# Attention and an MLP woven on one core: a round of maxima moved ahead of the score pair behind the products with v, and gaps of other lengths

## The chip, the core and the metric

The kernel runs on one core of a Trainium2 chip. TensorE (PE in the profile; PEld is its weight load) multiplies matrices, VectorE (DVE) and ScalarE (ACT) read its results from PSUM, GpSimd (POOL) works on SBUF alone, and SyncE (SP) issues most transfers. The metric is the device time of one execution in microseconds (us), the median of several runs. Lower is better.

## What is computed

Attention with 32 heads of 18 columns over 2048 tokens, and a channel MLP on the same tokens, mixed by a gate for each token:

```python
qkv = (x @ wqkv).reshape(B, S, 3, H, Dh)             # S 2048, D 576, H 32, Dh 18
p = softmax(einsum("bhqd,bhkd->bhqk", q, k) * scale)
a = einsum("bhqk,bhkd->bhqd", p, v) -> (B, S, D) @ wo
h = gelu(layernorm(x) @ w1 + b1)                     # F 4608
b = h @ w2 + b2
g = sigmoid((x * gate_w).sum(-1))
out = g * a + (1 - g) * b
```

## The kernel before

A first stage (about 250 us) projects q, k and v and normalises x. Then comes the main loop (lines 1273 to 1309), on which everything below turns; its last periods and a tail behind it hold the projection with wo.

**The loop.** 32 units (a pair of heads and half of the queries) of 16 steps each. A step is one block of 128 keys against 1024 queries. Two steps, an even and an odd one, make a period: from one block of products with v to the next. TensorE's order is the order in which the program is written, and into the loop's own work the MLP's matmuls are woven in pieces.

- **Score pair** (`s2`, line 243): two matmuls (L251) for two heads, side by side on the two halves of the array's rows, 512 queries, into the tile `pss`. Its pool `ps_s2` (line 1051) has one buffer of two banks. One ACTIVATE (L253) takes exp of all 1024 columns. A step has two such pairs, so a period has four: one ahead of the products with v, one behind them, and two in the odd step. A pair cannot begin before the exp of the pair ahead has read `pss`.
- **Products with v** (`pv`, line 257): 16 matmul records (L268) once in a period, on column tiles of 32, where all other matmuls of the loop run on row tiles of 64.
- **Round of maxima** (`s1_round`, line 192): exp needs the maximum of each row, so the scores of a later unit are computed once ahead: two matmuls (L202) into two of the three banks of `ps_s1` (line 93), and two VectorE reductions (L204), each of which frees its bank. A period has four rounds: 1024 in all.
- **Up slots** (`h_pair`, line 478): two matmuls (L502), 27 slots for one pair of hidden tiles. **Output slots** (`out_pair`, line 596): two matmuls (L630), 24 slots for 128 tokens. At slot 12 the two halves swap their column halves ("turn"): a semaphore wait on TensorE, and ahead of it one round of maxima is lent (`lend_round`, line 317); the round that the loop would put next is left out then (`loop_round`, line 322).

**The gaps.** `fill` (line 1249) is called three times in a period: with share 0 at the end of the even step, with share 1 in the middle of the odd one, with share 2 at its end. While rounds are left it runs one piece of the MLP (`atom`, line 730), up to the next cut. The sets `ends` (lines 495 to 499 and 609) say after which slots a piece is cut. With lines 499 and 609 a period holds 24 output slots in pieces of 7, 8 and 9, or up slots in pieces of 4, 5, 5 and then 4, 5, 4. Where an up pair is run in one period, its pieces are 9, 9 and 9.

**The order in an even step**: a round, the score pair, the products with v, the second score pair, a round, the gap (lines 1288 to 1309, with the round behind `s2(u, kc, 1)` at line 1307). In an odd step: a round, the score pair, the gap, a round, the score pair, the gap. In the first 8 steps, line 1299 puts one round more behind the products with v, ahead of the second score pair.

Of the kernel before, what the change touches and what calls it, by code (L numbers as in the profile page):

```python
# [58 lines left out]
def gated_mix_kernel(ctx: ExitStack, tc: tile.TileContext, x, wqkv, wo, w1, b1, w2, b2, gate_w, out):  # L59
# [39 lines left out]
    def psum(pool):  # L99
        return pool.tile([P, TB], F32, name="ps")  # L100
# [18 lines left out]
    def defer(n, fn):  # L119
        later.append((slot[0] + n, fn))  # L120
# [49 lines left out]
    def load_q(u):  # L170
        pair, half = unit(u)
        qa = QA[u % 3]
        for h in range(2):
            d0 = (2 * pair + h) * DH
            for i, part in enumerate((0, 0, 1)):
                r = 64 * h + i * DH
                dma_r(nc.sync, qa[r:r + DH, :], qk_scr[part, d0:d0 + DH, half * HALF:(half + 1) * HALF])

    def load_k(pair, c0=0, c1=S):
        ka = KA[pair % 3]  # L180
        for h in range(2):
            d0 = D + (2 * pair + h) * DH
            for i, part in enumerate((0, 1, 0)):
                r = 64 * h + i * DH
                dma_r(nc.sync, ka[r:r + DH, c0:c1], qk_scr[part, d0:d0 + DH, c0:c1])

    def load_v(pair):
        nc.sync.dma_start(VT[pair % 2], v_scr[:, :, pair, :].rearrange("k p e -> p k e"))
# [54 lines left out]
    def s2(u, kc, qb):  # L243
        qa, ka = QA[u % 3], KA[UNITS[u][0] % 3]
        n = u * NT + kc
        if n < 2 and qb == 0:
            RING.insert(n, pp.tile([P, 2, 2, TB], F32, name="p"))
        ps = ps_s2.tile([P, 2, TB], F32, name="pss")
        for h in range(2):
            r0 = 64 * h  # L250
            nc.tensor.matmul(ps[:, h, :], ka[r0:r0 + 56, kc * P:(kc + 1) * P], qa[r0:r0 + 56, qb * TB:(qb + 1) * TB],  # L251
                             start=True, stop=True)
        nc.scalar.activation(RING[n % 3][:, qb], ps, AF.Exp, scale=SCALE)  # L253
# [3 lines left out]
    def pv(n):  # L257

        u, kc = divmod(n, NT)
        if kc == 0:  # L260
            OB[u] = psum(ps_o)
        v = VT[UNITS[u][0] % 2]
        for c in (n, n + 1):
            for qb in range(2):
                for h in range(2):
                    r = 32 * (2 * h + qb)
                    k = c % NT
                    nc.tensor.matmul(OB[u][r:r + 32, :], v[:, k, 19 * h:19 * h + 32], RING[c % 3][:, qb, h, :],  # L268
                                     start=(k == 0), stop=(k == NT - 1))
        if kc == NT - 2:  # L270
            o_store(u, OB.pop(u))
# [35 lines left out]
    def next_round():  # L307
        if rounds:
            u, r = rounds.pop()
            s1_round(u, r)  # L310
            if r == NR - 1:
                defer(1, lambda: s1_finish(u))
# [4 lines left out]
    def lend_round():  # L317
        if rounds and not lent[0]:
            next_round()
            lent[0] = 1  # L320

    def loop_round():
        if lent[0]:
            lent[0] = 0
        else:
            next_round()

    def mlp():
# [90 lines left out]
        def ready(table, key):  # L419
            while key not in table:  # L420
                bg.pop(0)[1]()
            return table[key]
# [35 lines left out]
        def cuts(n, pieces):  # L458

            return {(k * n + pieces - 1) // pieces for k in range(1, pieces)}  # L460
# [3 lines left out]
        def free_pool():  # L464

            if rounds:
                return ps_w
            turns[0] += 1
            return (ps_s1, ps_w)[(turns[0] - 1) // 2 % 2]
# [8 lines left out]
        def h_pair(q, last, inner=False):  # L478
# [16 lines left out]
            ends = cuts(27, (5, 5, 4)[piece[0]] if last else (3, 5, 4)[piece[0]])  # L495
            if (last or spent[0] > behind[0] + AHEAD) and piece[0] == 0 and not late:

                ends = {4, 9, 14, 18, 23}
            for k, (w_, s_, c) in enumerate(slots):
                for h in range(2):  # L500
                    r = slice(64 * h, 64 * h + 64)
# [94 lines left out]
        def out_pair(i, t, acc):  # L596

            tb, g = seq[i]
            tok = slice(t * P, (t + 1) * P)
            cs = [slice(nn * ND, (nn + 1) * ND) for nn in range(2)]  # L600
            bare = not rounds

            def add(ps, base):
                for nn in range(2):
                    dst = acc[:, t, cs[nn]]
                    nc.vector.scalar_tensor_tensor(dst, ps[nn][:, :ND], 0.5, b2b[:, cs[nn]] if base else dst,  # L606
                                                   op0=ALU.mult, op1=ALU.add)
            ps = [psum(free_pool()) for _ in range(2)]
            ends = {7, 15} if piece[0] == 0 else cuts(24, (3, 2, 1)[piece[0]])
            k = 0  # L610
            for turn in range(2):
                if turn == 1 and bare:
                    add(ps, g == 0)
                    ps = [psum(free_pool()) for _ in range(2)]
                elif turn == 1:
                    if 3 * G not in ends:
                        lend_round()
                    turned[0] += 2
                    nc.tensor.wait_ge(turn_sem, turned[0])
                for j in ORDER:  # L620
                    while (i, j) not in HT:
                        cut[0] = 3
                        yield 0
                    hh, hl = HT[i, j]
                    w_ = ready(W2, (i * (G // 2) + j // 2, j % 2))
                    for h_, p_ in ((hh, 0), (hh, 1), (hl, 0)):
                        for h in (0, 1) if turn == 0 else (1, 0):
                            r = slice(64 * h, 64 * h + 64)
                            nn = h ^ turn
                            mm = nc.tensor.matmul(ps[nn][:, :ND], h_[r, tok], w_[p_][r, cs[nn]],  # L630
                                                  start=(k == 0 or bare and k == 3 * G), stop=(k == 6 * G - 1 or bare and k == 3 * G - 1))
                            if bare:
                                continue
                            if k == 3 * G - 1:
                                mm.then_inc(turn_sem, 1)
                                tc.no_tile_sem_insts.add(mm.ins.name)
                                tc.add_to_no_dep_group(f"turn{turned[0]}", mm.ins)
                            elif k == 3 * G and h == 0:
                                tc.declare_fence(mm.ins, group=f"turn{turned[0] - 2}")
                        k += 1  # L640
                        if k < 6 * G:
                            if k in ends:
                                cut[0] = 1
                            yield 131
            add(ps, g == 0 and not bare)
            if g == NG - 1:
                tt = TBS[tb] * 4 + t
                nc.gpsimd.tensor_scalar(acc[:, t, :], acc[:, t, :], gate1[:, tt:tt + 1], 1.0, op0=ALU.mult, op1=ALU.mult)
                defer(12 if tb < NB - 1 else 4, lambda: nc.sync.dma_start(b_scr[tt * P:(tt + 1) * P, :], acc[:, t, :]))
            cut[0] = 2  # L650
            yield 131
# [74 lines left out]
    piece = [0]  # L726
# [546 lines left out]
    for u in range(NU):  # L1273
        for kc in range(NT):
            step = u * NT + kc
            if kc == 1:
                if u + 2 < NU:
                    load_q(u + 2)
                if u % 2 == 0 and u // 2 + 1 < NPAIR - 1:
                    load_k(u // 2 + 1)  # L1280
                    load_v(u // 2 + 1)
                elif u == NU - 5:
                    load_k(NPAIR - 1)
                elif u == NU - 4:
                    load_v(NPAIR - 1)
            at[0] = step

            loop_round()
            s2(u, kc, 0)
            run_due(462.0)  # L1290
            if kc % 2:
                fill(step, 1)
            elif step > 0:
                pv(step - 2)
                while ROWS:
                    ROWS.pop(0)()
                run_due(2080.0)
                if step <= 2 * LEAD:
                    next_round()
            else:  # L1300
                fill(step, 2)
            if kc % 2:
                loop_round()
            s2(u, kc, 1)
            if kc % 2 == 0:

                loop_round()
            run_due(462.0)
            fill(step, 2 if kc % 2 else 0)
    pv(NSTEP - 2)  # L1310
# [28 lines left out]
```

## Time and profile before

| | |
|---|---|
| median of 3 runs | 2296.48 us (2295.54 to 2302.27) |
| the profiled execution, its own time | 2296.81 us |
| span of its trace | 2295.0 us |
| matmuls L502, L630, L251, L202, L268: busy | 522.8, 881.4, 488.3, 479.9, 523.7 us |
| exp (ACT L253): 1024 of mean 1025 ns | 1049.7 us busy |
| maxima (DVE L204): 2048 of mean 683 ns | 1284.8 us busy |

The rows of the timeline give the start in us from the span's start, the length, engine, line, operation, what it writes and reads, how many were merged, and in brackets how long the engine stood idle before it and what ended that. A matmul's length is modelled: in a stream of 512 columns it reads 0.40 us while the next begins 0.23 us after it; where its weights came late it reads 0.45 to 0.51 us.

### The profile page before, as it was taken

The numbers are of one execution on the slowest core, as the hardware profiler recorded it, in microseconds if no ns is written. First come the engines' busy times: TensorE is split into PE (matmuls) and PEld (weight loads), VectorE is DVE, ScalarE is ACT, GpSimd is POOL, SyncE is SP. The second block draws the span as 40 slices with busy tenths as digits, with TensorE's granted clock in tenths as the row PEclk, the third lists the DMA queues.
The fourth block names the chain that finished last, engine by engine and source line by source line (L and its number), as shares of the span: only waits on it lengthen the run. The fifth ranks groups of instructions, "written<-read, shape, count | busy, mean of one in ns | idle before, by whom it ended". The sixth has DMA issues, their size and how long they took to land.

```text
span 2295.0 us, 50552 instructions
## 1 busy us (share of the span) xinstructions
PE 2273.5 (99%) x20601; PEld 1620.6 (71%) x20601; DVE 1654.4 (72%) x2921; ACT 1379.2 (60%) x1631; POOL 946.6 (41%) x936
## 2 busy tenths in 40 slices
PE   8999999999999999999999999999999999999999
PEld 7878667666666767767667666767676766667668
DVE  5675777777777777777777777777777777777545
ACT  4223676766766666666666666666666666666661
POOL 4002466566653434443444344434444443333320
PEclk9999999999999999999999999999999999999999
DMA  7755645445473524232364324243465233322346
GB/s 243 252 186 187 197 147 170 161 137 169 142 192 133 166 85 130 97 119 98 93 170 150 116 94 139 80 118 118 120 164 155 96 120 112 105 97 105 112 160 207
DMA packets 160654, 323.58 MB, mean 141 GB/s; under 512 B 56062, under 2 KB 83618, under 8 KB 149586
## 3 DMA queue, kind: packets, MB, share of 16 engines
q1 hardware_dynamic: 156582, 313.57, 43.6%
q10 hardware_dynamic: 3840, 6.78, 0.8%
q8 instruction: 162, 2.65, 0.5%
q14 instruction: 70, 0.57, 0.1%
HBM read 229.07 MB, written 95.16 MB: 141 GB/s over the span
## 4 chain that ended last, share of the span: by engine, by line
PE 90%; POOL 4%; DVE 2%; ACT 2%; DMA 1%; issue 1%; SPq 0%; ACTq 0%; POOLq 0%; DVEq 0%
PE ps L268 19%; PE ps L630 19%; PE ps L502 17%; PE pss L251 13%; PE ps L202 11%; PE ps L904 5%; PE ps L1211 2%; PE ps L922 2%; POOL zz L159 1%; POOL w L159 1%; POOL hl L159 1%; DVE m L204 1%; PE ps L819 1%; DMA wraw<-in_B_w_dram 1%; ACT p L253 0%
## 5 line engine op out<-in xcount | busy, mean ns | idle before, releaser
L204 DVE TENSOR_REDUCE m<-ps 128x1 f32<-128x512 f32 x2048 | 1284.8, 683 | 341.8 <-PE ps L202 339.1
L253 ACT ACTIVATE p<-pss 128x1024 f32<-128x1024 f32 x684 | 701.1, 1025 | 436.6 <-PE pss L251 422.5
L502 PE MATMUL ps<-big,w 64*128 64x512 f32 x3834 | 515.2, 392 | 0.1
L159 POOL TENSOR_SCALAR zz<-zz 128x512 f32<-128x512 f32 x272 | 168.4, 619 | 807.7 <-ACT zz L588 743.8
L630 PE MATMUL ps<-w,hh 64*128 64x288 f32 x4352 | 498.2, 297 | 2.8 <-ACT z L525 2.1
L251 PE MATMUL pss<-qa,ka 56*128 56x512 f32 x2048 | 488.3, 442 | 4.9 <-ACT p L253 2.3
L202 PE MATMUL ps<-ka,qa 54*128 54x512 f32 x2048 | 479.9, 413 | 3.1 <-DVE m L204 1.7
L253 ACT ACTIVATE ring<-pss 128x1024 f32<-128x1024 f32 x340 | 348.6, 1025 | 221.1 <-PE pss L251 213.6
L502 PEld LDWEIGHTS ps<-big,w 64*128 64x128 f32 x3834 | 392.5, 185 | 57.7 <-ACT vt L933 0.3
L630 PEld LDWEIGHTS ps<-w,hh 64*128 64x128 f32 x4352 | 397.9, 186 | 32.2 <-ACT z L525 2.5
L251 PEld LDWEIGHTS pss<-qa,ka 56*128 56x128 f32 x2048 | 197.0, 184 | 256.9 <-ACT p L253 120.5
L159 POOL TENSOR_TENSOR zz<-zz,z 128x512 f32<-128x512 f32 x280 | 361.3, 1291 | 34.8 <-ACT zz L590 10.5
L630 PE MATMUL ps<-w,hl 64*128 64x288 f32 x2176 | 348.9, 292 | 0.0
L268 PE MATMUL ps<-p,vt 128*32 128x512 f32 x2736 | 344.6, 598 | 0.0
L202 PEld LDWEIGHTS ps<-ka,qa 54*128 54x128 f32 x2048 | 265.4, 185 | 34.8 <-DVE m L204 12.1
L630 PEld LDWEIGHTS ps<-w,hl 64*128 64x128 f32 x2176 | 233.2, 186 | 0.4
L159 POOL TENSOR_TENSOR w<-x,w 128x576 fp32r<-128x576 f32 (+1 forms) x34 | 68.3, 2010 | 303.7 <-ACT w L398 299.4
L159 POOL TENSOR_TENSOR hl<-zz,hh 128x512 fp32r<-128x512 f32 x134 | 174.1, 1300 | 17.2 <-DMA vt<-v_scr 4.3
L268 PE MATMUL ps<-ring,vt 128*32 128x512 f32 x1360 | 179.1, 598 | 0.0
L606 DVE SCALAR_TENSOR_TENSOR x<-ps,x 128x288 f32<-128x288 f32 x270 | 110.9, 452 | 89.7 <-PE ps L630 89.7
L268 PEld LDWEIGHTS ps<-p,vt 128*32 128x32 f32 x2736 | 71.5, 109 | 147.2 <-issue 147.0
L904 PE MATMUL ps<-big,wqk 128*128 128x512 f32 x504 | 123.6, 401 | 0.0
(122 smaller groups left out, 1407.7 us busy)
## 6 DMA issues: line engine op xcount, KB each, us to landing
w<-w_scr SPq DMA_DIRECT2D x54, 1152.0 KB
w<-w_scr SPq DMA_DIRECT2D x108, 576.0 KB
w_scr<-w SPq DMA_DIRECT2D x18, 1152.0 KB
w_scr<-w SPq DMA_DIRECT2D x36, 576.0 KB
qa<-qk_scr SPq DMA_DIRECT2D x192, 72.0 KB
ka<-qk_scr SPq DMA_DIRECT2D x90, 144.0 KB
x<-in_B_w_dram SPq DMA_DIRECT2D x34, 288.0 KB
qk_scr<-hh SPq DMA_DIRECT2D x36, 256.0 KB
```

What stands on the lines that cost most here:

```text
L159: fn(*args, **kw)
L202: nc.tensor.matmul(ps, qa[r0:r0 + 54, t * P:(t + 1) * P], ka[r0:r0 + 54, kb * TB:(kb + 1) * TB], start=True, stop=True)
L204: nc.vector.tensor_reduce(M4[u][:, h, t, kb:kb + 1], ps, axis=AX.X, op=ALU.max)
L251: nc.tensor.matmul(ps[:, h, :], ka[r0:r0 + 56, kc * P:(kc + 1) * P], qa[r0:r0 + 56, qb * TB:(qb + 1) * TB], start=True, stop=True)
L253: nc.scalar.activation(RING[n % 3][:, qb], ps, AF.Exp, scale=SCALE)
L268: nc.tensor.matmul(OB[u][r:r + 32, :], v[:, k, 19 * h:19 * h + 32], RING[c % 3][:, qb, h, :], start=(k == 0), stop=(k == NT - 1))
L502: nc.tensor.matmul(ps[h], wt[w_][r, c, :], Y[s_][r, c, :], start=(k == 0), stop=(k == 26))
L606: nc.vector.scalar_tensor_tensor(dst, ps[nn][:, :ND], 0.5, b2b[:, cs[nn]] if base else dst, op0=ALU.mult, op1=ALU.add)
L630: mm = nc.tensor.matmul(ps[nn][:, :ND], h_[r, tok], w_[p_][r, cs[nn]], start=(k == 0 or bare and k == 3 * G), stop=(k == 6 * G - 1 or bare ...
L904: nc.tensor.matmul(ps, w_[:, c, ms], big[:, s_, :], start=(k == 0), stop=(k == len(prods) - 1))
L922: nc.tensor.matmul(ps[:, :ND], big[:, s_, tok], w_[:, c, cs], start=(k == 0), stop=False)
L1211: nc.tensor.matmul(ps[t, n][:, :ND], OT[b][3][:, s_, tok], w_part(w_, c)[:, cs], start=(c == 0 and k == 0), stop=(c == 4 and k == 1))
```

## The change

In the even step the round of maxima that stood behind the second score pair now stands ahead of it, right behind the products with v. The odd step is as it was. The gaps are cut elsewhere: output slots in 8, 8 and 8 instead of 7, 8 and 9, up slots in 5, 5, 4 and then 5, 4, 4.

```diff
@@ h_pair
             if (last or spent[0] > behind[0] + AHEAD) and piece[0] == 0 and not late:
-                ends = {4, 9, 14, 18, 23}
+                ends = {5, 10, 14, 19, 23}
@@ out_pair
-            ends = {7, 15} if piece[0] == 0 else cuts(24, (3, 2, 1)[piece[0]])
+            ends = {8, 16} if piece[0] == 0 else cuts(24, (3, 2, 1)[piece[0]])
@@ the loop
-            if kc % 2:
-                loop_round()
+            loop_round()
             s2(u, kc, 1)
-            if kc % 2 == 0:
-                loop_round()
             run_due(462.0)
```

Only TensorE's order changes; the rows of VectorE, ScalarE, GpSimd and SyncE stand as before. Of the 255 periods, counted in TensorE's order, 135 hold 24 output slots (the first three of them with the extra round), 82 hold 13 or 14 up slots (41 of each), 27 hold 27 up slots, and 11 at the end have three rounds or none. These counts are the same in both kernels.

First place, TensorE in a period with output slots, from the products with v (`p` is the tile of exps, `vt` v) to the odd step's first score pair. `ps<-ka,qa` is a round of maxima, `pss<-qa,ka` a score pair, `w_3111,hh` and the like output slots. Before:

```order
L268 MATMUL ps<-p,vt_109 32x512 x8
L251 MATMUL pss<-qa_103,ka_106 128x512 x2
L202 MATMUL ps<-ka_107,qa_105 128x512 x2
L630 MATMUL ps<-w_3111,hh 128x288 x4
L630 MATMUL ps<-w_3111,hl 128x288 x2
L630 MATMUL ps<-w_3124,hh 128x288 x4
L630 MATMUL ps<-w_3124,hl 128x288 x2
L630 MATMUL ps<-w_3159,hh 128x288 x2
L202 MATMUL ps<-ka_107,qa_105 128x512 x2
L251 MATMUL pss<-qa_103,ka_106 128x512 x2
```

The same stretch of the changed kernel:

```order
L268 MATMUL ps<-p,vt_109 32x512 x8
L202 MATMUL ps<-ka_107,qa_105 128x512 x2
L251 MATMUL pss<-qa_103,ka_106 128x512 x2
L630 MATMUL ps<-w_3111,hh 128x288 x4
L630 MATMUL ps<-w_3111,hl 128x288 x2
L630 MATMUL ps<-w_3124,hh 128x288 x4
L630 MATMUL ps<-w_3124,hl 128x288 x2
L630 MATMUL ps<-w_3159,hh 128x288 x4
L202 MATMUL ps<-ka_107,qa_105 128x512 x2
L251 MATMUL pss<-qa_103,ka_106 128x512 x2
```

Between the two score pairs stood a round, 7 output slots and a round; now there stand 8 slots and a round.

Second place, TensorE in a period with up slots (`big,w_2961`), from the score pair behind the products with v to the one ahead of the next. Before:

```order
L251 MATMUL pss<-qa_103,ka_106 128x512 x2
L202 MATMUL ps<-ka_106,qa_104 128x512 x2
L502 MATMUL ps<-big,w_2961 128x512 x8
L202 MATMUL ps<-ka_106,qa_104 128x512 x2
L251 MATMUL pss<-qa_103,ka_106 128x512 x2
L502 MATMUL ps<-big,w_2961 128x512 x10
L202 MATMUL ps<-ka_106,qa_104 128x512 x2
L251 MATMUL pss<-qa_103,ka_106 128x512 x2
L502 MATMUL ps<-big,w_2961 128x512 x10
L202 MATMUL ps<-ka_107,qa_105 128x512 x2
L251 MATMUL pss<-qa_103,ka_106 128x512 x2
```

The same stretch of the changed kernel, from the round that now stands right behind the products:

```order
L202 MATMUL ps<-ka_106,qa_104 128x512 x2
L251 MATMUL pss<-qa_103,ka_106 128x512 x2
L502 MATMUL ps<-big,w_2961 128x512 x10
L202 MATMUL ps<-ka_106,qa_104 128x512 x2
L251 MATMUL pss<-qa_103,ka_106 128x512 x2
L502 MATMUL ps<-big,w_2961 128x512 x10
L202 MATMUL ps<-ka_106,qa_104 128x512 x2
L251 MATMUL pss<-qa_103,ka_106 128x512 x2
L502 MATMUL ps<-big,w_2961 128x512 x8
L202 MATMUL ps<-ka_107,qa_105 128x512 x2
L251 MATMUL pss<-qa_103,ka_106 128x512 x2
```

One round went from between the first two score pairs to ahead of them, and one up slot from the last gap to the first.

Third place, TensorE around the turn of an output period, from the odd step's first score pair to the second (the first slots behind the round, the rows of `w_3111`, are those behind the turn). Before:

```order
L251 MATMUL pss<-qa_103,ka_106 128x512 x2
L630 MATMUL ps<-w_3159,hh 128x288 x2
L630 MATMUL ps<-w_3159,hl 128x288 x2
L630 MATMUL ps<-w_3145,hh 128x288 x4
L630 MATMUL ps<-w_3145,hl 128x288 x2
L202 MATMUL ps<-ka_107,qa_105 128x512 x2
L630 MATMUL ps<-w_3111,hh 128x288 x4
L630 MATMUL ps<-w_3111,hl 128x288 x2
L251 MATMUL pss<-qa_103,ka_106 128x512 x2
```

In the changed kernel:

```order
L251 MATMUL pss<-qa_103,ka_106 128x512 x2
L630 MATMUL ps<-w_3159,hl 128x288 x2
L630 MATMUL ps<-w_3145,hh 128x288 x4
L630 MATMUL ps<-w_3145,hl 128x288 x2
L202 MATMUL ps<-ka_107,qa_105 128x512 x2
L630 MATMUL ps<-w_3111,hh 128x288 x4
L630 MATMUL ps<-w_3111,hl 128x288 x2
L630 MATMUL ps<-w_3124,hh 128x288 x2
L251 MATMUL pss<-qa_103,ka_106 128x512 x2
```

Five slots, the lent round and three slots became four slots, the round and four slots.

## The prediction, before the result was known

> **What bounds the kernel now.** I read the page first: the span and the engines' shares.
>
> ```profile
> span 2295.0 us, 50552 instructions
> PE 2273.5 (99%) x20601; PEld 1620.6 (71%) x20601; DVE 1654.4 (72%) x2921; ACT 1379.2 (60%) x1631; POOL 946.6 (41%) x936
> ```
>
> TensorE counts as busy throughout. That share cannot tell whether it is held up, because a matmul that waits for its weights only reads longer. So I went on to the groups of weight loads, kept apart by form, and to the waits.
>
> ```profile
> L251 PEld LDWEIGHTS pss<-qa,ka 56*128 56x128 f32 x2048 | 197.0, 184 | 256.9 <-ACT p L253 120.5 <-ACT ring L253 61.7 <-ACT zz L588 47.8
> L202 PEld LDWEIGHTS ps<-ka,qa 54*128 54x128 f32 x2048 | 265.4, 185 | 34.8 <-DVE m L204 12.1 <-issue 3.6 <-DVE big L835 1.1
> PEld pss L251 <- ACT zz L588: 47.8, 57, 0.8
> ```
>
> The weight loads that wait are those of the score pairs, and ScalarE ends the wait: exp 182.2 us, another activation 47.8 us in 57 cases. The rounds of maxima wait little. Then the timeline of one output period, ScalarE alone:
>
> ```profile
> 1006.13 1.02 ACT L253 ACTIVATE p<-pss 128x1024 f32<-128x1024 f32 x1 [0.72 <-PE pss L251]
> 1008.41 1.03 ACT L253 ACTIVATE p<-pss 128x1024 f32<-128x1024 f32 x1 [1.26 <-PE pss L251]
> 1010.16 1.02 ACT L253 ACTIVATE p<-pss 128x1024 f32<-128x1024 f32 x1 [0.72 <-PE pss L251]
> 1011.83 1.03 ACT L253 ACTIVATE p<-pss 128x1024 f32<-128x1024 f32 x1 [0.65 <-PE pss L251]
> 1013.52 1.02 ACT L253 ACTIVATE ring<-pss 128x1024 f32<-128x1024 f32 x1 [0.66 <-PE pss L251]
> ```
>
> From one exp to the next: 2.28 us across the products with v, then 1.75, 1.67 and 1.69; together 7.39, the period. TensorE in the same period:
>
> ```profile
> 1007.82 0.50 PE L251 MATMUL pss<-qa,ka 56*128 56x512 f32 x2
> 1008.15 0.40 PE L202 MATMUL ps<-ka,qa 54*128 54x512 f32 x2
> 1008.38 0.44 PE L630 MATMUL ps<-w,hh 64*128 64x288 f32 x4
> ...
> 1009.32 0.51 PE L202 MATMUL ps<-ka,qa 54*128 54x512 f32 x2
> 1009.56 0.50 PE L251 MATMUL pss<-qa,ka 56*128 56x512 f32 x2
> 1009.83 0.37 PE L630 MATMUL ps<-w,hh 64*128 64x288 f32 x2
> ...
> 1010.50 0.52 PE L202 MATMUL ps<-ka,qa 54*128 54x512 f32 x2
> 1010.78 0.53 PE L630 MATMUL ps<-w,hh 64*128 64x288 f32 x4
> ...
> 1011.28 0.45 PE L251 MATMUL pss<-qa,ka 56*128 56x512 f32 x2
> ...
> 1012.76 0.40 PE L202 MATMUL ps<-ka,qa 54*128 54x512 f32 x2
> 1013.00 0.42 PE L251 MATMUL pss<-qa,ka 56*128 56x512 f32 x2
> 1013.34 0.64 PE L268 MATMUL ps<-p,vt 128*32 128x512 f32 x4
> 1011.23 0.19 PEld L251 LDWEIGHTS pss<-qa,ka 56*128 56x128 f32 x2
> ```
>
> The short intervals are a closed chain. The exp at 1010.16 ends at 1011.18; at 1011.23 the next pair's weights load (last row), its matmuls follow, and its exp starts at 1011.83, 0.65 after the exp ahead ended. With 1.02 for the exp itself that makes 1.67 to 1.69 from exp to exp when nothing but the chain binds: the **floor**, about 1.68. What TensorE can lay between two pairs is worth little more than that: a round or a pair costs 0.23 us (1008.15 to 1008.38), an output slot 0.134 (7 in the 0.94 us from 1008.38 to 1009.32). In the last interval, pair, 9 slots and round make 1.67. So the kernel stands on two bounds at once: TensorE's stream just fills a chain that ScalarE closes three times in each period. Only the long interval has room, where the products with v (1.85 us) cover exp.
>
> **The change, step by step.** Matmuls, reductions and activations are the same in number and kind, and no transfer is issued elsewhere. What counts is in which interval the work lies. A round goes from the first short interval, where it covered the chain, into the long one, where exp is covered anyway.
>
> *Long interval.* It grows by one round. Before shows exactly this order in its first periods, where an extra round follows the products (the first rows are ScalarE's, the last two TensorE's):
>
> ```profile
> 268.26 1.02 ACT L253 ACTIVATE p<-pss 128x1024 f32<-128x1024 f32 x1 [0.65 <-PE pss L251]
> 270.78 1.02 ACT L253 ACTIVATE p<-pss 128x1024 f32<-128x1024 f32 x1 [1.50 <-PE pss L251]
> 270.00 0.51 PE L202 MATMUL ps<-ka,qa 54*128 54x512 f32 x2
> 270.34 0.40 PE L251 MATMUL pss<-qa,ka 56*128 56x512 f32 x2
> ```
>
> 2.52 from exp to exp instead of 2.28: **+0.24**. The round takes over the late weights behind the products (0.34 to the next start, as the pair's 0.33 from 1007.82 to 1008.15), so nothing is saved there. Here the pair's exp starts 0.44 after it, against 0.59 for a pair with late weights, 0.10 of which is the load (0.33 to the next start in place of 0.23); so up to 0.05 may come back.
>
> *First short interval, 1.75.* Without the round there is pair, 8 slots, round: 0.23 + 8 x 0.134 + 0.23 = 1.53, less than the floor. It falls to 1.68 and no further, **-0.07**. The 0.07 above the floor was VectorE's: the round at 1009.32 reads 0.51, because its second half needed the bank of the round at 1008.15. That wait goes, since the moved round lies 1.6 us ahead; what is late next is exp.
>
> *Second short interval, 1.67.* 4 + 4 slots instead of 5 + 3. The lent round comes 1.18 after the round at 1009.32 and waits for the same kind of bank (0.52 instead of 0.40), and one slot more now lies behind it. That round's start, from the pair behind the products, moves from 1.50 to 0.34 + 0.23 + 8 x 0.134 = 1.64; 1.96 from it to the second odd pair (1009.32 to 1011.28), plus one slot of 0.134, gives 3.73. The chain alone would have that pair at 3.46 + 0.24 - 0.07 = 3.63, or 0.05 later if the load is exposed. So between 0 and 0.1 is added; I take **+0.01**, as the chain's own rows are the closer ones.
>
> *Third short interval, 1.69.* 8 slots instead of 9: 1.53 of work under a floor of 1.68: **0**. The missing slot gains nothing.
>
> An output period comes to +0.18. Periods with up slots, ScalarE's rows of one with 13 and of one with 14:
>
> ```profile
> 920.75 1.02 ACT L253 ACTIVATE ring<-pss 128x1024 f32<-128x1024 f32 x1
> 923.03 1.03 ACT L253 ACTIVATE ring<-pss 128x1024 f32<-128x1024 f32 x1 [1.27 <-PE pss L251]
> 924.84 1.02 ACT L253 ACTIVATE p<-pss 128x1024 f32<-128x1024 f32 x1 [0.78 <-PE pss L251]
> 926.51 1.03 ACT L253 ACTIVATE p<-pss 128x1024 f32<-128x1024 f32 x1 [0.66 <-PE pss L251]
> ...
> 846.28 1.02 ACT L253 ACTIVATE p<-pss 128x1024 f32<-128x1024 f32 x1 [1.27 <-PE pss L251]
> 848.03 1.03 ACT L253 ACTIVATE p<-pss 128x1024 f32<-128x1024 f32 x1 [0.72 <-PE pss L251]
> ```
>
> 2.28, then 1.81 and 1.67 in the first, 1.75 in the second. An up slot is 0.234 (9 in 2.11 us, rows below), so the new gaps of 5 hold 0.23 + 5 x 0.234 + 0.23 = 1.63 and those of 4 hold 1.40: all under the floor. Change: 0.24 - 0.13 = +0.11 with 13 slots, 0.24 - 0.07 = +0.17 with 14. Where a period holds 27 up slots, the chain is slack:
>
> ```profile
> 1015.77 2.26 PE L502 MATMUL ps<-big,w 64*128 64x512 f32 x18
> 1017.88 0.40 PE L202 MATMUL ps<-ka,qa 54*128 54x512 f32 x2
> ...
> 1015.80 1.03 ACT L253 ACTIVATE ring<-pss 128x1024 f32<-128x1024 f32 x1 [1.26 <-PE pss L251]
> 1018.61 1.03 ACT L253 ACTIVATE p<-pss 128x1024 f32<-128x1024 f32 x1 [1.78 <-PE pss L251]
> ```
>
> 2.81 from exp to exp, of which 1.78 idle: these 27 periods only swap 0.23 between two intervals, 0. The 11 at the end have no round to move, and the first three output periods are left at 0, since their three rounds in a row wait for banks in either order.
>
> **The sum.** 132 x 0.18 = 23.8, 41 x 0.17 = 7.0, 41 x 0.11 = 4.5: 35.3 us. On the profiled execution's 2296.81 (0.33 above the median) that is **2332 us**, 1.5% slower.
>
> Low end: 0.05 less in each of the 214 periods takes 10.7, and in the 57 cases where another activation holds the pair, the 0.18 may be hidden, 10.3; 2311. High end: the first short interval keeps its 0.07, and the turn adds its full 0.1: 132 x 0.34 + 82 x 0.24 = 64.6, so 2361; both at once lie far from the rows, and I stop at 2350.
>
> **The rivals.**
>
> *Nothing moves: 2297.* TensorE is 99% busy with the same instructions. It speaks against this that the waits stand in the weight loads, 256.9 us in front of L251. The Trainium skill says the same in "Perfetto Trace Analysis", Identifying the Most-Contended Engine: matmul busy time is no good measure of how near the engine is to its limit.
>
> *Faster: 2286.* If VectorE's banks, not exp, are what binds, the moved round sits in the shadow of the products and frees its banks early, and 0.05 us (0.10 on one of a round's two halves) is gained in each of 214 periods: 10.7. It decides at 1.53 us: exp and the way back to TensorE would have to be done by then, or the slots behind a waiting pair would have to overtake it. The rows above, with 0.65 to 0.78 idle between two exps, speak against the first. On the second, the Trainium skill ("TensorE: Matmul & The Clock Gate", Step-by-step: what each phase is for) says that matmuls stay in program order and only weight loads are pulled ahead. The trace agrees: the slots behind the pair at 1009.56, which was held for its exp, begin at 1009.83, none ahead of it.
>
> *Slower by more, above 2350:* the full price of the turn, above.
>
> **How the numbers follow.** The forecast with its bounds: 0.80. More than 2350: 0.04. Between 2304 and 2311: 0.04, where more is hidden than I found. Nothing: 0.06. Faster: 0.06. A difference of 0.3%, 6.9 us, is about the least that a measurement of this kernel tells from none; so slower 0.88, same 0.06, faster 0.06. The range 2311 to 2350 leaves out 0.20.
>
> **What would show it.** Right: ScalarE's rows of an output period read about 2.52, 1.68, 1.69, 1.68 from exp to exp; the waits of L251's weight loads for exp grow by tens of us, L202's for VectorE shrink; periods with 27 up slots last as long as before. Wrong: short intervals well under 1.65, a long one of 2.3, or rounds behind the products that wait for a bank.

## The result, and the profile after

| | median us | range | runs |
|---|---|---|---|
| before | 2298.18 | 2295.54 to 2302.27 | 4 |
| the changed kernel | 2332.23 | 2331.59 to 2335.55 | 4 |

The ratio is 1.0149, with a 95% interval of 1.013 to 1.0169. The profiled execution of the changed kernel took 2331.98 us, 35.2 more than the one of before. Its page begins:

```profile
span 2330.2 us, 50552 instructions
PE 2306.9 (99%) x20601; PEld 1565.6 (67%) x20601; DVE 1672.8 (72%) x2921; ACT 1379.8 (59%) x1631; POOL 947.5 (41%) x936
```

The instructions are the same in number, and TensorE again reads 99%. Where the time goes shows in the intervals from exp to exp. ScalarE in the output period that was shown of before, from the timeline:

```profile
1020.94 1.02 ACT L253 ACTIVATE p<-pss 128x1024 f32<-128x1024 f32 x1 [0.72 <-PE pss L251]
1023.46 1.02 ACT L253 ACTIVATE p<-pss 128x1024 f32<-128x1024 f32 x1 [1.50 <-PE pss L251]
1025.14 1.03 ACT L253 ACTIVATE p<-pss 128x1024 f32<-128x1024 f32 x1 [0.66 <-PE pss L251]
1026.85 1.03 ACT L253 ACTIVATE p<-pss 128x1024 f32<-128x1024 f32 x1 [0.68 <-PE pss L251]
1028.53 1.03 ACT L253 ACTIVATE ring<-pss 128x1024 f32<-128x1024 f32 x1 [0.65 <-PE pss L251]
```

That is 2.52, 1.68, 1.71 and 1.68, together 7.59; before it was 7.39. TensorE in the same period (the last two rows are weight loads):

```profile
1022.63 0.50 PE L202 MATMUL ps<-ka,qa 54*128 54x512 f32 x2
1022.97 0.40 PE L251 MATMUL pss<-qa,ka 56*128 56x512 f32 x2
...
1024.26 0.41 PE L202 MATMUL ps<-ka,qa 54*128 54x512 f32 x2
1024.54 0.50 PE L251 MATMUL pss<-qa,ka 56*128 56x512 f32 x2
...
1025.41 0.53 PE L202 MATMUL ps<-ka,qa 54*128 54x512 f32 x2
...
1026.30 0.45 PE L251 MATMUL pss<-qa,ka 56*128 56x512 f32 x2
...
1024.54 0.19 PEld L251 LDWEIGHTS pss<-qa,ka 56*128 56x128 f32 x2 [0.21 <-ACT p L253]
1027.93 0.18 PEld L251 LDWEIGHTS pss<-qa,ka 56*128 56x128 f32 x2 [0.21 <-ACT p L253]
```

The moved round (1022.63) has the late weights behind the products, and the pair follows it 0.34 later. The pair at 1024.54 comes only 0.28 behind a round that needs 0.23: its weights waited for the exp that ended at 1024.48. The same happens in the third interval (1027.93), where TensorE now has less than 1.68 us of work.

The 255 periods of each trace were taken by kind, without those that hold a transpose of the maxima (L219). The whole is a mean, from the first product with v to the next period's. The four intervals from exp to exp are medians, so they do not add up to it:

| period (count) | before: whole, [long, first, second, third] | after | difference |
|---|---|---|---|
| output (116) | 7.413 [2.283, 1.743, 1.681, 1.681] | 7.570 [2.521, 1.679, 1.704, 1.677] | +0.157 |
| 14 up slots (37) | 7.356 [2.119, 1.745, 1.644, 1.675] | 7.480 [2.355, 1.638, 1.648, 1.674] | +0.124 |
| 13 up slots (35) | 7.435 [2.289, 1.795, 1.680, 1.683] | 7.555 [2.515, 1.696, 1.681, 1.685] | +0.120 |
| 27 up slots (22) | 10.215 | 10.216 | 0.001 |

Together with the 26 output and up periods that hold a transpose (+5.7) and the first periods (+2.2), both below, that is 34.9 of the 35.2 us.

The weight loads, grouped by form, read otherwise than expected:

```profile
L202 PEld LDWEIGHTS ps<-ka,qa 54*128 54x128 f32 x2048 | 225.1, 184 | 218.1 <-DVE m L204 149.8 <-issue 22.9 <-DVE dn L291 21.8
L251 PEld LDWEIGHTS pss<-qa,ka 56*128 56x128 f32 x2048 | 199.7, 185 | 149.9 <-ACT p L253 97.9 <-ACT ring L253 46.2
```

L251's idle time fell by 107 us and L202's rose by 183. That is bookkeeping: the first weight load behind the products stands idle for 0.84 us in every period, which is the products' own run. This load was L251's and is now L202's (one row of before, one of after):

```profile
1007.82 0.19 PEld L251 LDWEIGHTS pss<-qa,ka 56*128 56x128 f32 x2 [0.84 <-ACT p L253]
```

```profile
1022.63 0.19 PEld L202 LDWEIGHTS ps<-ka,qa 54*128 54x128 f32 x2 [0.84 <-DVE m L204]
```

The view of the waits (total us, count, longest us) mixes this load with the others. Two rows of before and two of after:

```profile
PEld pss L251 <- ACT p L253: 120.5, 218, 1.4
PEld pss L251 <- ACT ring L253: 61.7, 110, 1.0
```

```profile
PEld pss L251 <- ACT p L253: 97.9, 365, 1.0
PEld pss L251 <- ACT ring L253: 46.2, 175, 0.8
```

Taken load by load from the traces, 158 of the 328 waits of before (133 of their 182 us) are this load behind the products; so 170 waits of 49 us in all were for exp. Of the 540 after, 9 are (7.5 of 144 us); so 531 waits of 137 us are for exp. They are three times as many and about as long as before, 0.26 us in the mean against 0.29.

### The profile page after: what moved, and what is told of

It is laid out like the page before. It is cut to its first block, busy times and chain, and to the rows that moved or that the text cites. A ratio compares the mean times of both kernels' runs of the same rounds, so it can differ in the third digit from the quotient of the medians.

```text
span 2330.2 us, 50552 instructions
## 1 busy us (share of the span) xinstructions
PE 2306.9 (99%) x20601; PEld 1565.6 (67%) x20601; DVE 1672.8 (72%) x2921; ACT 1379.8 (59%) x1631; POOL 947.5 (41%) x936
## 4 chain that ended last, share of the span: by engine, by line
PE 92%; DVE 3%; POOL 2%; ACT 1%; DMA 1%; issue 1%; SPq 0%; ACTq 0%; DVEq 0%; POOLq 0%
PE ps L268 19%; PE ps L630 18%; PE ps L502 18%; PE ps L202 13%; PE pss L251 13%; PE ps L904 4%; PE ps L1211 3%; PE ps L922 2%; POOL zz L159 1%; DVE m L204 1%; POOL hl L159 1%; PE ps L819 0%; ACT p L253 0%; POOL w L159 0%; DMA p<-in_A_wqkv_dram 0%
## 5 line engine op out<-in xcount | busy, mean ns | idle before, releaser
L204 DVE TENSOR_REDUCE m<-ps 128x1 f32<-128x512 f32 x2048 | 1304.8, 684 | 356.6 <-PE ps L202 339.1
L502 PE MATMUL ps<-big,w 64*128 64x512 f32 x3834 | 505.5, 392 | 0.1
L202 PE MATMUL ps<-ka,qa 54*128 54x512 f32 x2048 | 474.8, 429 | 5.1 <-DVE m L204 3.4
L251 PE MATMUL pss<-qa,ka 56*128 56x512 f32 x2048 | 467.3, 440 | 5.2 <-ACT p L253 3.1
L502 PEld LDWEIGHTS ps<-big,w 64*128 64x128 f32 x3834 | 364.8, 185 | 76.4 <-ACT vt L933 0.3
L630 PEld LDWEIGHTS ps<-w,hh 64*128 64x128 f32 x4352 | 388.9, 186 | 25.6 <-ACT z L525 2.5
L202 PEld LDWEIGHTS ps<-ka,qa 54*128 54x128 f32 x2048 | 225.1, 184 | 218.1 <-DVE m L204 149.8
L630 PE MATMUL ps<-w,hl 64*128 64x288 f32 x2176 | 340.9, 293 | 0.0
L251 PEld LDWEIGHTS pss<-qa,ka 56*128 56x128 f32 x2048 | 199.7, 185 | 149.9 <-ACT p L253 97.9
L630 PEld LDWEIGHTS ps<-w,hl 64*128 64x128 f32 x2176 | 224.7, 186 | 3.5
```

What stands on the lines that cost most here:

```text
L202: nc.tensor.matmul(ps, qa[r0:r0 + 54, t * P:(t + 1) * P], ka[r0:r0 + 54, kb * TB:(kb + 1) * TB], start=True, stop=True)
L204: nc.vector.tensor_reduce(M4[u][:, h, t, kb:kb + 1], ps, axis=AX.X, op=ALU.max)
L502: nc.tensor.matmul(ps[h], wt[w_][r, c, :], Y[s_][r, c, :], start=(k == 0), stop=(k == 26))
```

## The experiments

Theory A is the forecast's: the chain of pair, exp and free bank sets a floor under the short intervals, and a round that leaves the first of them lengthens the period. Its rivals: the gaps do it, or VectorE's banks, or the moved row of instructions itself.

**The order alone.** The changed kernel with the old gaps:

```diff
-                ends = {5, 10, 14, 19, 23}
+                ends = {4, 9, 14, 18, 23}
...
-            ends = {8, 16} if piece[0] == 0 else cuts(24, (3, 2, 1)[piece[0]])
+            ends = {7, 15} if piece[0] == 0 else cuts(24, (3, 2, 1)[piece[0]])
```

> The round stands right behind the products with v, as in the changed kernel, but the gaps are those of before (7, 8, 9 output slots; 4, 5, 5 and 4, 5, 4 up slots). Theory A (exp closes the three short intervals at 1.68 us, a round moved into the long interval is paid in full): all of the cost is here, 2329 to 2334 us; the first short interval would hold 1.40 us of work and still take 1.68. Theory B (the new gaps cost the time, by moving slots to where the turn and the banks make them late): about 2298.

Measured: 2331.19 us (2329.43 to 2331.77), ratio 1.0146 (1.0131 to 1.0162), as theory A expected. The output period is 7.560, with 2.517, 1.679, 1.682 and 1.682. The moved round costs all of it; the new gaps on top add 1 us or nothing. The turn's 1.682 here against 1.704 in the changed kernel prices the gap of 8 in front of the turn at 0.02.

**The gaps alone.** The kernel before with the new gaps (the diff above, turned round).

> Order of before, gaps of the changed kernel. Theory A: this costs too, by another road: the first short interval now holds 0.23 + 0.23 + 8 x 0.134 + 0.23 = 1.77 us in output periods (was 1.75) and 1.86 with 5 up slots (was 1.75 to 1.81), and the third is under the floor with one slot less, so what is added in the first is not given back: up periods about +0.15 (82 of them, 12 us), output periods +0.02 from the first interval and 0 to 0.15 from the turn (132 of them, 3 to 20 us); 2313 to 2332. Theory B (gaps are what the change costs): 2332. Theory C (only the order counts): 2298.

Measured: 2325.75 us (2325.3 to 2326.17), ratio 1.0124 (1.0109 to 1.0139), within what theory A expected. ScalarE in the same output period:

```profile
1016.81 1.02 ACT L253 ACTIVATE p<-pss 128x1024 f32<-128x1024 f32 x1 [0.72 <-PE pss L251]
1019.10 1.02 ACT L253 ACTIVATE p<-pss 128x1024 f32<-128x1024 f32 x1 [1.27 <-PE pss L251]
1020.87 1.02 ACT L253 ACTIVATE p<-pss 128x1024 f32<-128x1024 f32 x1 [0.74 <-PE pss L251]
1022.68 1.03 ACT L253 ACTIVATE p<-pss 128x1024 f32<-128x1024 f32 x1 [0.78 <-PE ps L630]
1024.35 1.02 ACT L253 ACTIVATE ring<-pss 128x1024 f32<-128x1024 f32 x1 [0.65 <-PE pss L251]
```

The long interval stays at 2.29. One slot more beside a round in the first interval, which was full, and one more in front of the turn cost 0.03 and 0.12 (medians 1.769 and 1.802 in output periods); the slot that left the third interval gives nothing back, since exp holds it at 1.67. So either half of the change alone costs nearly as much as both, and the costs do not add. In the old order the new gaps overfill an interval; in the new order the round has made room for them, at the price that it already cost.

**Exp in two halves.** If exp's chain is the floor, a chain with a bank of its own for each head might be shorter. In the kernel before, and then in the changed one, the pair writes two tiles of one bank, each with its own exp:

```diff
-        ps = ps_s2.tile([P, 2, TB], F32, name="pss")
+        ps = [ps_s2.tile([P, TB], F32, name="pss") for h in range(2)]
...
-        nc.scalar.activation(RING[n % 3][:, qb], ps, AF.Exp, scale=SCALE)
+        for h in range(2):
+            nc.scalar.activation(RING[n % 3][:, qb, h], ps[h], AF.Exp, scale=SCALE)
...
-    ps_s2 = ctx.enter_context(tc.tile_pool(name="ps_s2", bufs=1, space=PSUM))
+    ps_s2 = ctx.enter_context(tc.tile_pool(name="ps_s2", bufs=2, space=PSUM))
```

> Order and gaps of before, but each pair has two tiles of one bank and each its own exp of 512 columns, so that a bank is free about 0.4 us sooner. Theory A: the floor falls from 1.68 to about 1.3 and no interval is held by exp: output periods gain 0.06, up periods 0.1 to 0.3 (a gap of 4 then takes 1.40 instead of 1.68); 2270 to 2285. Theory C (the price lies on TensorE itself, in changing between row and column tiles or in late weights): no gain, 2298 or more, since ScalarE has some 200 us more to do.

> Order and gaps of the changed kernel with the exp split as in the run ahead. Theory A: without the floor the moved round costs nothing, and the wait for VectorE's bank in the first short interval is gone: as fast as the split kernel with the order of before, or up to 20 us faster, 2255 to 2285; the sign of the change turns. Theory C: the changed order stays 34 us dearer than the run ahead.

Measured: 2282.02 us (2279.74 to 2282.33), ratio 0.9932 (0.9917 to 0.9946), with the old order, which is the fastest complete kernel of this study; 2311.39 (2307.45 to 2313.29), ratio 1.0056 (1.0039 to 1.0073), with the new one. The first lies in the range expected. But the change still costs 29.4 us, so the expectation for the second kernel fell. Period means from the one to the other: 7.221 to 7.220 with 13 up slots, where the change now costs nothing, 7.320 to 7.472 with 14, and 7.374 to 7.523 with output slots. Four of the second kernel's ScalarE rows in an output period, each two halves, and two of its pairs on TensorE:

```profile
790.11 1.09 ACT L254 ACTIVATE ring<-pss 128x512 f32<-128x512 f32 x2 [1.57 <-PE pss L251]
791.64 1.08 ACT L254 ACTIVATE p<-pss 128x512 f32<-128x512 f32 x2 [0.44 <-PE pss L251]
793.40 1.09 ACT L254 ACTIVATE p<-pss 128x512 f32<-128x512 f32 x2 [0.68 <-PE pss L251]
794.94 1.08 ACT L254 ACTIVATE p<-pss 128x512 f32<-128x512 f32 x2 [0.45 <-PE pss L251]
789.67 0.40 PE L251 MATMUL pss<-qa,ka 56*128 56x512 f32 x2
791.21 0.54 PE L251 MATMUL pss<-qa,ka 56*128 56x512 f32 x2
```

The intervals are 1.53, 1.76 and 1.54. The first and the third are as long as the 1.53 of work in them, and the second with 13 up slots, where the work is 1.40, has a median of 1.398: the floor is well below 1.68. But pairs still wait for exp. The pair at 789.67 is followed by both halves of exp, which end at 790.11 + 1.09 = 791.20. The next pair's first half starts at 791.21, 0.23 behind the round, and the pair reads 0.54, not 0.40, because its second half starts later. In the 116 output periods the second half of a pair starts 0.053 us (median) after its exp's end in the first interval and 0.057 in the third; a whole pair of the changed kernel has 0.068 and 0.056. So the pair is complete only when the *last* bank is free, and two halves need 1.09 us where one ACTIVATE needs 1.02. In the turn's interval it is 0.295: exp no longer holds it there, something else does, and it stays at 1.76. How much of the 29.4 us comes from these late second halves is not shown. Of the 15.6 us that the split gains in the old order, about half lies in the 35 periods with 13 up slots (7.435 to 7.221, 7.5 us).

**Exp at half length.** To shorten the chain itself, exp is taken of the first head's 512 columns only; the other head's exp is left out, and its half of the tiles holds what was written there once. All matmuls and reductions stay. The kernel before and the changed one:

```diff
             RING.insert(n, pp.tile([P, 2, 2, TB], F32, name="p"))
+            nc.gpsimd.memset(RING[n], 1.0)
...
-        nc.scalar.activation(RING[n % 3][:, qb], ps, AF.Exp, scale=SCALE)
+        nc.scalar.activation(RING[n % 3][:, qb, 0], ps[:, 0, :], AF.Exp, scale=SCALE)
```

> Order and gaps of before; exp is taken of the first head's 512 columns alone (the second head's tiles keep a constant), so that an exp takes 0.6 us instead of 1.02 and frees both banks then. The split of the runs ahead did not do that: its second half still came free 1.68 us after the pair. Theory A (the time from a pair to the end of its exp is the floor): floor 1.25 us, no interval held by exp, 2268 to 2284 us; what is left is VectorE's bank in the first short interval (1.75). Theory C (the price lies on TensorE itself): 2298.

> Order and gaps of the changed kernel with the same half exp (the second head's exp is left out). Theory A as first put (only exp holds the intervals): as fast as its twin with the order of before, within 5 us. Theory A2 (behind exp stands a second bound, VectorE's banks at the lent round and the turn, which delays output periods by 0.1 more when the round ahead of it starts 0.13 later, while up periods gain the 0.05 of the bank wait): 0 to 17 us over the twin, most likely 9. Theory C: 34 us over the twin.

Measured: 2274.78 us (ratio 0.9899, 0.9884 to 0.9913) and 2274.91 us (0.99, 0.9885 to 0.9915). The first lies in theory A's range, and the second, level with its twin, in those of A and A2 alike. With exp short, the change costs 0.13 us in place of 34. This decides between theory A and the rivals that leave exp out. ScalarE in an output period of the changed kernel with half of exp:

```profile
1001.42 0.60 ACT L254 ACTIVATE p<-pss 128x512 f32<-128x512 f32 x1 [0.94 <-PE pss L252]
1003.94 0.60 ACT L254 ACTIVATE p<-pss 128x512 f32<-128x512 f32 x1 [1.93 <-PE pss L252]
1005.48 0.60 ACT L254 ACTIVATE p<-pss 128x512 f32<-128x512 f32 x1 [0.95 <-PE pss L252]
1007.28 0.60 ACT L254 ACTIVATE p<-pss 128x512 f32<-128x512 f32 x1 [1.20 <-PE pss L252]
1008.80 0.60 ACT L254 ACTIVATE ring<-pss 128x512 f32<-128x512 f32 x1 [0.92 <-PE pss L252]
```

2.52 is as long as ever, but the first and the third short interval fall to 1.54 and 1.52: the pair, 8 slots and a round that the forecast put at 1.53. So the floor of 1.68 was exp's. The second interval, 1.80 where the old order with half of exp has 1.63, shows the other bound. Here the lent round waits, and VectorE, in the same period, has no gap in front of it:

```profile
1005.74 0.68 PE L202 MATMUL ps<-ka,qa 54*128 54x512 f32 x2
1003.85 3.81 DVE L204 TENSOR_REDUCE m<-ps 128x1 f32<-128x512 f32 x6
```

There are six reductions in a row, one every 0.6 us; the round reads 0.68 in all because its second half waits for a bank. The zero is therefore a balance: output periods still lose 0.084 us each to the turn (7.336 to 7.420; 116 of them, 9.7 us), and periods with 14 and 13 up slots gain 0.108 and 0.102 (37 x 0.108 + 35 x 0.102 = 7.6). All 255 periods together still lose about 5 us, and the stretches ahead of them and behind them are about as much shorter, for a reason that no run shows.

**Maxima at half length too.** The same two kernels, where in addition the maxima are taken over the first 256 of each 512 columns:

```diff
-            nc.vector.tensor_reduce(M4[u][:, h, t, kb:kb + 1], ps, axis=AX.X, op=ALU.max)
+            nc.vector.tensor_reduce(M4[u][:, h, t, kb:kb + 1], ps[:, :TB // 2], axis=AX.X, op=ALU.max)
```

> As the half exp with the order of before, and the maxima too are taken of 256 of each 512 columns, so that a reduction takes about 0.4 us instead of 0.68 and frees its bank earlier. Theory A2: the first short interval falls from 1.75 to about 1.65, the lent round no longer waits; 10 to 20 us under the twin with whole maxima. Theory C: no difference to that twin.

> Order and gaps of the changed kernel with half exp and half maxima (the second head's exp and half of the columns of each maximum are left out). Theory A2: neither exp nor banks bind, TensorE's stream alone counts, and it is the same work: within 5 us of its twin with the order of before. Theory C: 34 us over the twin.

Measured: 2249.46 us (ratio 0.9788, 0.9772 to 0.9805), 25 us under its twin with whole maxima, more than the 10 to 20 expected, and 2250.3 us (0.9793, 0.9778 to 0.9807), within the 5 us of its twin that theory A2 expected. The output periods are 7.266 and 7.271, with the turn's interval at 1.658 in both. In both kernels exp is done 0.43 us or more ahead of the next pair in each short interval of an output period (medians). So with neither wait TensorE takes 7.27 for a period in either order: the row of instructions itself costs nothing, and the old order stood 0.15 above it and the new one 0.30.

**Two rounds behind the products.** If one round moved costs 0.24 in the long interval and frees nothing, a second one should cost that again. In the changed kernel, the round ahead of the even step's first pair goes behind that pair, in front of the products:

```diff
-            loop_round()
+            if kc % 2:
+                loop_round()
             s2(u, kc, 0)
+            if kc % 2 == 0:
+                loop_round()
```

> The changed kernel, and in the even step the round of maxima ahead of the first score pair goes behind it too, to right in front of the products with v: a second round moves from a short interval (the third) into the long one. Theory A (a short interval takes 1.68 us whatever it holds, what goes into the long one is paid in full): the long interval grows from 2.52 to 2.76, the third stays at 1.68 with 1.30 of work; 214 x 0.235 = 50 us over the changed kernel, 2376 to 2385. Rival (the price belongs to a round behind the products, not to the interval that it leaves): no further cost, about 2332.

Measured: 2385.51 us (2384.01 to 2387.25), ratio 1.0384 (1.0366 to 1.0401), half a microsecond over the 2376 to 2385 that theory A expected. Its rival falls. ScalarE in the same output period:

```profile
1038.38 1.02 ACT L253 ACTIVATE p<-pss 128x1024 f32<-128x1024 f32 x1 [0.72 <-PE pss L251]
1041.14 1.03 ACT L253 ACTIVATE p<-pss 128x1024 f32<-128x1024 f32 x1 [1.73 <-PE pss L251]
1042.82 1.02 ACT L253 ACTIVATE p<-pss 128x1024 f32<-128x1024 f32 x1 [0.66 <-PE pss L251]
```

2.76 where there were 2.52 and 2.28, and then the floor again. The second round costs more (53 us against 34) since the interval that it left stood on the floor already and gave nothing back; the first one still brought 0.06 to 0.11 (first interval, medians).

**The transpose behind the moved round.** Output periods that hold a transpose grew by 0.219 (16 of them), those with 13 up slots by 0.298 (6), and with 14 by 0.095 (4), more than the others in two of three kinds. There the changed kernel has transpose, round, pair. If the moved round waits there for the bank that the transpose takes, the order round, transpose, pair might take the wait away:

```diff
                 pv(step - 2)
+                loop_round()
                 while ROWS:
                     ROWS.pop(0)()
...
-            loop_round()
+            if kc % 2 or step == 0:
+                loop_round()
             s2(u, kc, 1)
```

> The changed kernel with the transpose of the maxima (L219, 32 in all, in 26 of the 214 bound periods) behind the moved round instead of ahead of it. In the changed kernel these periods grew by 0.10 to 0.30 us rather than by the 0.11 to 0.18 of the others. If that excess is a wait of the moved round for the bank that the transpose takes, these periods fall by 0.05 to 0.2 and the kernel by 1 to 4 us, to about 2329; if not, 2332.

Measured: 2336.78 us (2336.04 to 2337.61), ratio 1.0169 (1.0154 to 1.0184): 4.5 us slower, not faster. The expectation fell. In periods with 27 up slots, where exp leaves slack, the same move shows its bare price, 10.430 to 10.634: a transpose between a round and a pair costs 0.20 us. On that row bears what the Trainium skill says ("TensorEngine Tiling (Array Packing)", Key Properties), that a change of the tiling mode drains TensorE. Right behind the products, which are tiled by columns as the transposes are, the transpose adds no change of tiling; between a round and a pair it adds two. No run separates such a drain from weights that come late.

The traces show where the excess lies. In 9 of the 26 periods of the changed kernel the moved round's second half starts 0.37 to 0.60 us behind its first; these grew by 0.37 in the mean, the other 17 by 0.14, like periods without a transpose. The weight loads of one of the nine, from the transpose to the pair:

```profile
818.50 0.09 PEld L219 LDWEIGHTS ps<-ident,nm 128*32 128x32 f32 x1 [0.84 <-DVE m L204]
818.71 0.18 PEld L202 LDWEIGHTS ps<-ka,qa 54*128 54x128 f32 x1
819.15 0.18 PEld L202 LDWEIGHTS ps<-ka,qa 54*128 54x128 f32 x1 [0.26 <-DVE m L204]
819.15 0.29 PEld L251 LDWEIGHTS pss<-qa,ka 56*128 56x128 f32 x2
```

The transpose takes one of the same three banks as the rounds (`ps_s1`), so with the round it needs all three ahead of the pair, and one of them is still being reduced. With the places swapped the transpose waits instead: in the same period its load stands idle 0.41 until the reduction ends, and eight of the nine periods take as long in either order, within 0.05 us. So the expectation had the right wait, but the swap could not remove it. It is some 2 us (9 x (0.37 - 0.14)) of the 35.

## Why the prediction was right

The time, the sign and the mechanism were as forecast: 2332 us forecast, 2332.2 measured. The sum was 35.3 us and the traces differ by 35.2. By its steps:

- **Long interval, +0.24:** measured +0.238 in output periods (2.283 to 2.521), +0.236 and +0.226 in up periods. The first periods of before had shown this order already, and the value carried over.
- **First short interval, -0.07, to the floor:** -0.064 (1.743 to 1.679). With half of exp it fell to 1.54, with the full exp it did not; so the floor is exp's. That the 0.07 above it was VectorE's is shown too: in the old order with half of exp, half maxima take this interval from 1.746 to 1.632.
- **Second interval, +0.01:** +0.023, within the 0 to 0.1 of the bounds. Half of exp showed the lent round's bank as the next bound, and it is what the split ran into as well, as far as its rows tell.
- **Third interval, 0:** -0.004. The slot taken out gave nothing.
- **Output period, +0.18:** +0.157 by the means, 0.02 too much.
- **14 up slots, +0.17:** +0.124. The term was mis-sized. The row it used had its long interval at 2.28 and its first one at 1.75; the median period stood at 2.119 and 1.745, and its first interval fell by 0.107, to 1.638, not by 0.07 to 1.68. The floor is lower in these periods: with the order alone, where the first gap holds 1.40 us of work, the interval is 1.624. So 1.638 is the 1.63 of work that the prediction itself added up and set under a floor of 1.68. Why the floor is 0.05 lower there is not shown. **13 up slots, +0.11:** +0.120.
- **27 up slots, 0:** 0.001.
- **First output periods, left at 0:** wrong, about 2.2 us together. The three grew by 0.67 each (8.375 to 9.040), a fourth by 0.24. "Wait for banks in either order" was true, but where the wait lies decides. The first of them after, two rounds in a row behind the products, weight loads and the exp that follows:

```profile
272.21 0.29 PEld L202 LDWEIGHTS ps<-ka,qa 54*128 54x128 f32 x3 [0.84 <-DVE m L204]
273.50 0.18 PEld L202 LDWEIGHTS ps<-ka,qa 54*128 54x128 f32 x1 [0.99 <-DVE m L204]
274.27 1.02 ACT L253 ACTIVATE p<-pss 128x1024 f32<-128x1024 f32 x1 [2.78 <-PE pss L251]
```

The fourth half-round waits 0.99 for one of three banks, ahead of the pair, and ScalarE idles 2.78. In the old order that wait came behind the pair and ran beside its exp.

These errors go both ways: output and 14-slot periods were put at some 4 us too much, and what was left out, the first periods and the excess in those with a transpose, brought about that back. That the total is closer than its terms is luck.

One of the signs was named without asking whose idle time the weight loads carry. Without the load behind the products, L251's waits for exp grew by tens of us, as forecast (49 to 137); but L202's for VectorE, which were to shrink, hardly moved (8.7 to 10.7). With that load, the views show the reverse. The reading of before has the same flaw: of the 256.9 us in front of L251, 185 are the products' own run. The 57 cases in which another activation was said to hold the pair are all of this kind: 47.8 us, 0.84 each. So the low end, which let these cases hide 10.3 us, had no ground. The sum used none of it.

Of the rivals, "nothing moves" and "faster" fell with the time. "Faster" rested on VectorE's banks as the bound; with the full exp they held the first interval by 0.06 and the turn by 0.02, and the floor took over just below. "Above 2350" needed the turn's full 0.1, and it took 0.02.

## What to carry to other kernels

Where one engine's chain closes several times in a period, find for each interval whether the chain or the stream of work sets it: work moved out of an interval that then falls below the chain gives back only the part above it, and costs its full length where it goes. So the cheapest row lays just enough work into each link; here, gaps that are one slot too long cost nearly as much as a whole round moved out (28 us for the gaps alone, 34 for the round). Read such a change by the intervals, and by waits from which the instruction that comes first behind a block is left out: sums and counts by line both move with it.

## What the runs showed of the hardware

- Two exps of 512 columns read 595 ns each, but together 1.09 us, so the second is 0.495 behind the first. Two halves cost 0.07 us more than one exp of 1024 columns.
- A transpose between a round and a pair costs 0.20 us more than one right behind the products with v (10.430 to 10.634 us for a period with 27 up slots).
- TensorE's busy share is 99% in the changed kernel and in the split one that is 50 us faster:

```profile
span 2280.5 us, 50913 instructions
PE 2262.5 (99%) x20601; PEld 1660.0 (73%) x20601; DVE 1655.7 (73%) x2921; ACT 1436.5 (63%) x2655; POOL 946.6 (42%) x936
```

The Trainium skill ("Perfetto Trace Analysis", Identifying the Most-Contended Engine) names the busy share of the weight loads as a better measure. Among these three it agrees: 73% at 2280.5 us, 71% before, 67% after. Over all runs it does not: the split kernel with the new order reads 71% at 2311.5 us, as before does at 2295.0, and the order of the change with half of exp and of the maxima reads 69% at 2246.6 us.
